# Loading r and k of the first five stages in 1536 B rows, and turning them to head-dim rows on PE through a strided identity

## The chip, the cores and the metric

One core of one Trainium2 chip. Time is device time of one execution in microseconds (us), as the median of several executions. TensorE is called PE, VectorE DVE, ScalarE ACT, GpSimd POOL and SyncE SP. A kernel is compared with the kernel before in the same rounds and on the same chip; ratios are the mean time of one kernel's fast runs over that of the other's fast runs of the same rounds, so they are not quite the ratio of the medians quoted. A run that is more than 1.5% above the fastest of its kernel counts as slow and is left out of ratios.

## The reference, cut to what matters

A linear attention with decay runs over 768 tokens, 8 heads of 48 dims and 4 batches. A two-layer MLP with a leaky ReLU then runs on its 3072 rows.

```python
for t in range(S):                                    # B, H, S, D = 4, 8, 768, 48
    cur = einsum('bhd,bhe->bhde', u * k_t, v_t)       # the "bonus" of the token itself
    y[:, :, t] = einsum('bhd,bhde->bhe', r_t, state + cur)
    state = w * state + einsum('bhd,bhe->bhde', k_t, v_t)
x = y.transpose(0, 2, 1, 3).reshape(3072, 384)
h = x @ w_in                                          # 384 x 2048
out = maximum(0.01 * h, h) @ w_out                    # 2048 x 384
```

The inputs r, k and v lie in memory as [batch, head, token, dim]. For one token and one head there are 48 contiguous fp32 values, 192 B. Eight consecutive tokens of one head are 1536 contiguous bytes.

## The kernel before: what the change and the argument touch

The tokens are worked on in 24 *stages* of 128 tokens, numbered 0 to 23. In each stage r and k are scaled with powers of w, turned so that head dims lie on the partitions (kt), and used for scores, the masked product with v, and the state. Rows y are turned to xT, and the MLP takes them in groups of one or two stages.

```python
# load: partition = token; 128 tokens x 8 heads = 1024 rows of 192 B for each of r, k, v
a = src[b].rearrange("h t d -> t h d")[c * L:c * L + L, :, :]
SP.dma_start(vr.t[:, xi, :, :], a)
# scale (DVE): r * w^(t-128), k * w^(127-t), or the like for the odd stage of a pair
V.tensor_tensor(kq[:, :, 0:D], raw_rk, tab[l], ALU.mult)
# turn (PE): 8 transposes of two heads each, then eviction to kt (DVE or ACT)
PE.transpose(tv[:, 128 * i:128 * i + 128], kq.t[:, 2 * i:2 * i + 2, :], idn)
# scores from kt; y from the masked scores, v and the state; the state from kq (tokens on partitions)
# ... (cut)
```

The tables of powers of w are built at the start from a load of w that is spread over all partitions (192 KB written). The weights of the MLP are loaded by POOL in pieces, each released by an earlier load. All this is data for a small planner inside the program: it simulates the engines and the DMA queues with estimated times and writes down *one fixed order* of operations for each engine.

```python
WI = [4, 4, 8]        # pieces of w_in      WO = [8, 8]   # pieces of w_out
DMA_SEQ = 'st0 st1@w u@k0 uw st2@k0 st3 wi0@u wi1@wi0 wi2@r1 wo0@v3 wo1@wo0'   # x@y: x released by y
MOE_BANKS = 4         # PSUM banks the MLP may hold
...
for _ in range(PASSES):
    P, order = build(landing)             # plans the order, with the landing times of the last pass
    landing, made = P.execute(order)      # simulates it
```

During the first 14 us PE also runs warming matmuls on zeros where the plan has nothing for it.

## Time and profile before

| | before |
|---|---|
| median of 4 runs | 194.53 us (194.17 to 196.57) |
| span of the profiled run | 192.6 us |
| PE busy, idle | 173.0 us, 19.6 us |
| warming matmuls | 9.0 us |
| DVE, ACT, POOL busy | 139.7, 116.7, 78.9 us |
| DMA packets, of them under 512 B | 97,308, 92,296 |

First the page's view of the span in 40 slices of 4.8 us: busy tenths of PE, the granted clock of PE in tenths, the busy share of the DMA engines, and what they moved.

```profile
PE   7875950999999979899899999999999999999973
...
PEclk9999798599999999999999999999999999999999
DMA  5999999999029999999997969996250220110202
GB/s 107 203 164 181 167 206 196 201 189 192 2 85 241 160 223 233 247 192 194 187 200 150 200 112 227 199 177 163 54 118 22 58 82 0 44 43 0 85 0 82
```

The DMA engines are full from the second slice to the tenth, with a gap in the eleventh and twelfth. PE has holes in the sixth and seventh slice (24 to 34 us), and a low clock in the fifth, seventh and eighth.

Next the busy time of each engine by stretch. The columns are: stretch, its length, then busy us (and count) of PE, PE weight loads, DVE, ACT and POOL, then the granted clock, the DMA share and GB/s.

```profile
0.00:35.00 35.00, 22.88 (x272) 17.60 (x273) 19.23 (x44) 13.64 (x26) 8.99 (x19) 0.91 0.95 175
35.00:60.00 25.00, 25.00 (x264) 18.93 (x263) 20.15 (x28) 16.52 (x26) 10.59 (x12) 0.92 0.67 136
60.00:140.00 80.00, 76.64 (x810) 59.89 (x808) 73.29 (x94) 57.28 (x87) 57.66 (x47) 1.00 0.96 185
140.00:200.00 60.00, 48.45 (x436) 36.85 (x432) 26.98 (x36) 29.20 (x40) 1.66 (x2) 0.98 0.15 43
```

PE is idle for 35 - 22.88 = 12.1 us in the first stretch, 0 in the second, 3.4 in the third and, with the span's end at 192.6, 4.2 in the last. From 35 us on PE sets the pace; the start is where time lies.

What the hole is made of stands in the timeline: start, duration, engine, line, operation, and in brackets how long the engine had been idle and what released it.

```profile
18.55 0.71 SPq L554 DMA_DIRECT2D raw<-in_k_dram  x1
...
26.64 0.83 PE L845 MATMUL ps_g<-xT,win 128*128 128x128 bf16 x12
...
32.35 0.96 DVE L653 TENSOR_TENSOR kq<-raw,tab 128x768 bf16<-128x768 f32 x1 [5.95 <-DMA raw<-in_k_dram]
...
33.37 1.04 PE L670 MATMUL ps_g<-idn,kq 128*128 128x128 bf16 x8 [5.89 <-DVE kq L653]
```

PE did nothing between 27.4 and 33.4 us, because the scaled k and r of a stage came late. The load was issued by 19.3 us and k landed at 32.3. After the hole the clock is low: 0.62 of full speed between 35 and 40 us. The Trainium skill, "TensorE: Matmul & The Clock Gate", Part 1, says that PE drops to half rate after an idle window of about 3.4 us and needs as much busy time to come back; the trace agrees for this drop (5.9 us of idle time, then a mean of 0.62). By the trace's clock records PE ran at half speed from 32.0 to 38.8 us. Not every drop follows such a gap: another one, from 18.4 to 21.8 us, came after 3.4 us in which PE was busy for 1.6 us and never idle for more than 0.85 us at a time.

The queues, from the view of the DMA: packets, MB, and the time that the packets took as a share of 16 engines' span.

```profile
q1 hardware_dynamic: 92232, 18.95, 53.7%
...
q10 hardware_dynamic: 3312, 4.52, 7.1%
```

### The profile page before, as it was taken

The page shows a single profiled execution, that of the slowest core. Times are in us where ns is not written, and L with a number is a line of the kernel's source. Part 1 is how long each engine was busy: PE and PEld are TensorE (multiplying, and loading weights), DVE is VectorE, ACT ScalarE, POOL GpSimd, SP SyncE. Part 2 cuts the span into 40 slices and gives each one's busy share as a digit, 9 for nine tenths or more (in the row PEclk, how much of TensorE's full clock was granted, in tenths as well). Part 3 has the DMA queues.
Part 4 walks back from the last instruction along what each step waited for, and adds up shares of the span by engine and source line. Part 5 has one row for each costly group of instructions (what it writes and reads, how often), then busy time and mean ns, then how long its engine had stood idle before and what let it go on. Part 6 is the DMA issues. An engine that isn't in the chain of part 4 may idle for free.

```text
span 192.6 us, 4283 instructions
## 1 busy us (share of the span) xinstructions
PE 173.0 (90%) x1773; PEld 133.3 (69%) x1773; DVE 139.7 (73%) x199; ACT 116.6 (61%) x178; POOL 78.9 (41%) x78
## 2 busy tenths in 40 slices
PE   7875950999999979899899999999999999999973
PEld 5654840597668857767677778778678787796841
DVE  2567942658699989999978997988957847514532
ACT  3844510885746864953975848938939559295450
POOL 2052302820558898958865819956111000000000
PEclk9999798599999999999999999999999999999999
DMA  5999999999029999999997969996250220110202
GB/s 107 203 164 181 167 206 196 201 189 192 2 85 241 160 223 233 247 192 194 187 200 150 200 112 227 199 177 163 54 118 22 58 82 0 44 43 0 85 0 82
DMA packets 97308, 26.90 MB, mean 140 GB/s; under 512 B 92296, under 2 KB 96392, under 8 KB 97288
## 3 DMA queue, kind: packets, MB, share of 16 engines
q1 hardware_dynamic: 92232, 18.95, 53.7%
q0 software_dynamic: 1744, 3.15, 9.3%
q10 hardware_dynamic: 3312, 4.52, 7.1%
q8 instruction: 14, 0.23, 0.5%
q14 instruction: 6, 0.05, 0.1%
HBM read 20.84 MB, written 4.72 MB: 133 GB/s over the span
## 4 chain that ended last, share of the span: by engine, by line
PE 49%; POOL 12%; DVE 10%; DMA 10%; issue 6%; SPq 6%; ACT 4%; ACTq 0%; POOLq 0%; DVEq 0%
PE ps_g L900 23%; PE ps_g L845 19%; DMA raw<-in_v_dram 8%; POOL pr L712 5%; SPq L554 5%; POOL pu L710 4%; DVE gring L880 3%; POOL bv L716 3%; DVE at L746 2%; ACT h L874 2%; DMA lnw<-in_w_dram 2%; DVE kq L653 2%; PE ps_xy L728 2%; PE ps_g L806 1%; PE ps_g L762 1%
## 5 line engine op out<-in xcount | busy, mean ns | idle before, releaser
L845 PE MATMUL ps_g<-xT,win 128*128 128x256 bf16 (+1 forms) x624 | 73.6, 270 | 0.0
L900 PE MATMUL ps_g<-wout,gring 128*128 128x384 bf16 x384 | 67.9, 326 | 4.1 <-DVE gring L880 4.1
L859 ACT ACTIVATE gring<-ps_g 128x512 bf16<-128x512 f32 x96 | 53.3, 597 | 27.7 <-PE ps_g L845 24.5
L845 PEld LDWEIGHTS ps_g<-xT,win 128*128 128x128 bf16 x624 | 61.8, 115 | 2.3 <-issue 0.2
L900 PEld LDWEIGHTS ps_g<-wout,gring 128*128 128x128 bf16 x384 | 35.8, 98 | 27.0 <-DVE gring L880 5.9
L880 DVE TENSOR_TENSOR gring<-gring,h 128x2048 bf16<-128x2048 bf16 (+1 forms) x26 | 34.9, 1341 | 11.8 <-ACT h L874 11.7
L716 POOL TENSOR_TENSOR bv<-vb,b 128x384 bf16<-128x384 bf16 x20 | 20.8, 1038 | 42.4 <-DVE b L714 27.5
L874 ACT ACTIVATE h<-gring 128x2048 bf16<-128x2048 bf16 (+1 forms) x20 | 35.7, 1784 | 0.5
L653 DVE TENSOR_TENSOR kq<-raw,tab 128x768 bf16<-128x768 f32 x24 | 26.0, 1082 | 10.4 <-DMA raw<-in_k_dram 6.6
L746 DVE TENSOR_TENSOR at<-ps_xy,tri 128x1024 bf16<-128x1024 f32 x22 | 26.8, 1216 | 4.7 <-PE ps_xy L728 4.7
L712 POOL TENSOR_TENSOR pr<-pu,raw 128x384 f32<-128x384 f32 x20 | 29.2, 1461 | 1.2
L710 POOL TENSOR_TENSOR pu<-raw,ubc 128x384 f32<-128x384 f32 x20 | 22.8, 1138 | 12.2 <-DMA raw<-in_k_dram 12.2
L657 ACT ACTIVATE vb<-raw 128x384 bf16<-128x384 f32 x24 | 12.6, 525 | 12.4 <-DMA raw<-in_v_dram 11.6
L909 DVE COPY o<-ps_g 128x384 f32<-128x384 f32 x16 | 8.9, 557 | 11.7 <-PE ps_g L900 11.6
L769 DVE TENSOR_TENSOR y<-ps_g,bv 128x384 bf16<-128x384 f32 x24 | 13.2, 549 | 1.5 <-PE ps_g L762 1.3
L812 ACT ACTIVATE xT<-ps_g 128x384 bf16<-128x384 bf16 x14 | 6.8, 487 | 10.6 <-PE ps_g L806 10.6
L714 DVE TENSOR_REDUCE b<-pr 128x8 f32<-128x384 f32 x20 | 10.8, 542 | 2.8 <-POOL pr L712 2.6
L670 PE MATMUL ps_g<-idn,kq 128*128 128x128 bf16 x64 | 5.8, 242 | 7.0 <-DVE kq L653 7.0
L670 PEld LDWEIGHTS ps_g<-idn,kq 128*128 128x128 bf16 x64 | 4.5, 109 | 8.1 <-DVE kq L653 7.6
L924 PE MATMUL ps_g<-zer 128*128 128x256 bf16 x59 | 9.0, 314 | 1.1 <-DVE zer L506 1.1
L728 PE MATMUL ps_xy<-kt 48*128 48x128 bf16 x192 | 10.0, 226 | 0.1
L806 PE MATMUL ps_g<-idn,y 128*128 128x128 bf16 x72 | 8.0, 220 | 2.2 <-DVE y L769 2.1
(56 smaller groups left out, 114.3 us busy)
## 6 DMA issues: line engine op xcount, KB each, us to landing
raw<-in_r_dram SPq DMA_DIRECT2D x24, 192.0 KB, 3.9
raw<-in_k_dram SPq DMA_DIRECT2D x24, 192.0 KB, 4.0
raw<-in_v_dram SPq DMA_DIRECT2D x24, 192.0 KB, 4.1
out_dram<-o ACTq DMA_DIRECT2D x23, 192.0 KB, 3.0
wout<-in_moe_w_out_dram POOLq DMA_DIRECT2D x2, 768.0 KB, 10.4
win<-in_moe_w_in_dram POOLq DMA_DIRECT2D x2, 384.0 KB, 6.7
win<-in_moe_w_in_dram POOLq DMA_DIRECT2D x1, 768.0 KB, 10.4
kt<-kq SPq DMA_TRANSPOSE x16, 3.8
```

The costliest lines, as they stand in the source:

```text
L653: use(op("DVE", 1.0, lambda: V.tensor_tensor(kq.t[:, :, 0:D], vr.t[:, 0:2, :, :].rearrange("p a h d -> p (a h) d"), tab[l][:, :, :, :].rea ...
L710: use(op("POOL", 1.15, lambda: G.tensor_tensor(pu.t[:, :, :], vr.t[:, 1, :, :], ubc[:, :, :], ALU.mult), f"pu{n}", pr_a(n, 0.2), reads=[f_ ...
L712: use(op("POOL", 1.15, lambda: G.tensor_tensor(pr.t[:, :, :], pu.t[:, :, :], vr.t[:, 0, :, :], ALU.mult), f"pr{n}", pr_a(n, 0.3), reads=[f ...
L716: op("POOL", 1.1, lambda: G.tensor_tensor(bv.t[:, :].rearrange("p (h d) -> p h d", d=D), vb.t[:, :].rearrange("p (h d) -> p h d", d=D), bb ...
L728: o = PE.matmul(xy.t[:, 512 * s + 128 * i:512 * s + 128 * i + 128], kt.t[rows, HP + i, :], kt.t[rows, i, :], start=(i == 0), stop=True, sk ...
L746: op("DVE", 1.22, lambda: V.tensor_tensor(at.t[:, :, :], xy.t[:, :].rearrange("p (h t) -> p h t", t=128), tri_b.to_broadcast([128, H, 128] ...
L769: op("DVE", 0.55, lambda: V.tensor_tensor(ys.t[:, :], y.t[:, 0:DM], bv.t[:, :], ALU.add), f"ys{n}", pr_a(n, 0.5), reads=[y, bv], writes=[ys])
L845: o = PE.matmul(bk.t[:, 128 * T * f:128 * T * (f + 1)], w_in_block(s, j * per + f), xT[:, s, L * n0:L * n0 + L * T], start=(s == 0), stop= ...
L859: return A.activation(o_ap, i_ap, AF.Copy) if e == "ACT" else V.tensor_copy(o_ap, i_ap)
L874: return A.activation(o_ap, i_ap, AF.Copy, scale=LRELU_SLOPE)
L880: return V.tensor_tensor(flat(dst(j0, j + 1)), flat(dst(j0, j + 1)), h_ap, ALU.max)
L900: o = PE.matmul(bk.t[:, 0:DM], gring[:, n % NG, fb, :], wout[:, fb, :], start=(fb == 0), stop=(fb == NFB - 1))
```

## The change

The intent is to move the same bytes of r and k of stages 0 to 4 in fewer, longer rows while the DMA engines are full. A 1536 B row holds eight tokens of one head, so a partition is (group of eight tokens, head), which no later step can use directly. Hence new tables for that layout, 16 small matmuls for each of r and k that pick the heads out of the partitions with a strided slice of the identity, an eviction to kt, and for k a second transpose back to token rows, which the state needs.

```diff
-MOE_BANKS = 4                                 +MOE_BANKS = 3
-QKT_DMA_FROM = 8                              +QKT_DMA_FROM = 9
-LEAD = 4.0                                    +LEAD = 5.0
-WI = [4, 4, 8]                                +WI = [4, 4, 4, 4]
-WO = [8, 8]                                   +WO = [4, 4, 8]
-DMA_SEQ = 'st0 st1@w u@k0 uw st2@k0 st3 wi0@u wi1@wi0 wi2@r1 wo0@v3 wo1@wo0'
+DMA_SEQ = 'st0 uw wi0@r0 st1 st2@r0 wi1@v2 wi2 u@r1 w@v0 st3@r1 wi3@v3 wo0@r1 wo1@w wo2'
+NWIDE = 5
-MASK_SPLIT = 2                                +MASK_SPLIT = 0
... (the planner: a margin on landing times, and the mean over four more cases of DMA behaviour)
+        if NWIDE:                             # a small load of w, 48 values a partition, for the wide tables
+            o_wp = op("SP", ..., SP.dma_start(lnp, dram(w, 0, [[0, 16], [D, H], [1, D]])), ...)
... (wide tables: 4 products on DVE, 4 exponentials on ACT; the old tables come later)
+                    if wide:                  # n < NWIDE, r and k only
+                        a = dram(src, (b * H * S + c * L) * D, [[8 * D, 16], [S * D, H], [1, 8 * D]])
+                        return [SP.dma_start(vr.t[:, xi, :, :].rearrange("p h d -> p (h d)"), a)]
... (for x in r, k: kw = raw * wide table, on DVE or POOL)
+                        PE.matmul(tp.t[:, :], zer[:, 0:128], zer[:, :], start=True, stop=False)
+                        for s in range(2):
+                            for j in range(8):
+                                o = PE.matmul(tp.t[64 * s:64 * s + D, 64 * j:64 * j + 64], kw_.t[:, x, j, :],
+                                              idn[:, s:128:2], start=False, stop=True)
... (eviction to kt; for k: 4 transposes of kt back and an eviction to kq)
```

The left and right of a line in the first block stand for a removed and an added line. Several things change at once: row size, engine work, load order, weight pieces and the planner's settings.

More of the change, by code (lines that the diff above doesn't have):

```diff
@@ L28 @@
 NH = 3
-MOE_BANKS = 4
-QKT_DMA_FROM = 8
+MOE_BANKS = 3
+QKT_DMA_FROM = 9
 YT_DMA_FROM = 99
-LEAD = 4.0
+LEAD = 5.0
 PERIOD = 6.0
@@ L39 @@
 RING = 2250
-WI = [4, 4, 8]
-WO = [8, 8]
-DMA_SEQ = 'st0 st1@w u@k0 uw st2@k0 st3 wi0@u wi1@wi0 wi2@r1 wo0@v3 wo1@wo0'
+MARGIN = 0.5
+CASES = [(1.5, 1.08, 1.1, 2.4, 1.35, 1.0), (2.6, 1.0, 1.1, 2.0, 1.6, 1.06), (2.0, 0.95, 1.3, 2.8, 1.9, 1.03), (1.7, 1.04, 1.0, 1.6, 1.2, 0.98)]
+WI = [4, 4, 4, 4]
+WO = [4, 4, 8]
+DMA_SEQ = 'st0 uw wi0@r0 st1 st2@r0 wi1@v2 wi2 u@r1 w@v0 st3@r1 wi3@v3 wo0@r1 wo1@w wo2'
+NWIDE = 5
 BONUS_PE = 4
-MASK_SPLIT = 2
+MASK_SPLIT = 0
 KT_SPLIT = 4
-KQ_SPLIT = 0
+KQ_SPLIT = 1
 GA_ALT = 99
@@ L225, in schedule @@
                 if o.name in self.landing:
-                    o.done = o.end + self.landing[o.name]
+                    o.done = o.end + self.landing[o.name] + (MARGIN if o.name[:2] in ("ld", "wi", "wo") else 0.0)
                 else:
@@ L246, in schedule, with execute @@
         return order
-    def execute(self, order):
+    def execute(self, order, case=(2.0, 1.0, 1.0, 2.4, 1.35, 1.0)):
+        gap_w, cost_l, gap_l, gap_h, land, cost_w = case
         dmaq = {e: [o for o in order[e] if o.pk is not None] for e in ("SP", "POOL", "ACT")}
@@ L303, in issue @@
             heavy = e != "POOL" and any(x in rem and begin[x] <= fin + 1.1 for x in dmaq["POOL"])
-            begin[o] = fin + (2.0 if e == "POOL" else 2.4 if heavy else 1.1)
+            begin[o] = fin + (gap_w if e == "POOL" else gap_h if heavy else gap_l)
             rem[o] = float(o.pk[0])
@@ L322, in live_next @@
             if live:
-                per = sum(o.pk[1] for _, o in live) / 16000.0
+                per = sum(o.pk[1] * (cost_l if o.pk[1] < 50 else cost_w) for _, o in live) / 16000.0
                 t = now + min(rem[o] for _, o in live) * per
@@ L338, in execute @@
             live = [(e, o) for e, o in live if o is not None and o in begin and begin[o] <= now + 1e-9]
-            per = sum(o.pk[1] for _, o in live) / 16000.0
+            per = sum(o.pk[1] * (cost_l if o.pk[1] < 50 else cost_w) for _, o in live) / 16000.0
             for e, o in live:
@@ L344, in execute @@
                 if rem[o] < 1e-6:
-                    done[o] = t + LAND
+                    done[o] = t + land
                     landing[o.name] = done[o] - end[o]
@@ L427, in bass_rwkv5_eagle__then__act_leaky_relu_kernel @@
     lnw = SB("lnw", [128, H, D], FP32)
+    lnp = SB("lnp", [128, D], FP32)
+    row = SB("row", [128, 1], mybir.dt.int32)
+    rowf = SB("rowf", [128, 1], FP32)
+    cj = SB("cj", [128, 2, 2, 8], FP32)
+    tabw = [SB(f"tabw{i}", [128, 2, 8, D], FP32) for i in range(2)]
     ex = SB("ex", [128, 4], FP32)
@@ L437, in bass_rwkv5_eagle__then__act_leaky_relu_kernel @@
     idn = SB("idn", [128, 128])
-    zer = SB("zer", [128, 256])
+    zer = SB("zer", [128, 512])
     gring = SB("gring", [128, NG, NFB, 128])
@@ L444, in bass_rwkv5_eagle__then__act_leaky_relu_kernel @@
         "kt": SBN("kt", NKT, [128, 2 * HP, 128]),
+        "kw": SBN("kw", 2, [128, 2, 8, D]),
         "vb": SBN("vb", NVB, [128, DM]),
@@ L502, in build @@
         f_wo = [fixed(f"wo{i}") for i in range(len(WO))]
-        o_w = op("SP", 0.45, lambda: [SP.dma_start(lnw[:, :, :], dram(w, 0, [[0, 128], [D, H], [1, D]]))],
-                 "w", -200, writes=[f_lnw], pk=(128, 110), sem="w")
+        f_lnp, f_lnp2, f_row, f_rowf = [fixed(x) for x in ("lnp", "lnp2", "row", "rowf")]
+        f_cj = [fixed(f"cj{x}") for x in range(2)]
+        f_tabw = [[fixed(f"tabw{i}{x}") for x in range(2)] for i in range(2)]
+        if NWIDE:
+            o_wp = op("SP", 0.45, lambda: [SP.dma_start(lnp[:, :], dram(w, 0, [[0, 16], [D, H], [1, D]]))],
+                      "wp", -201, writes=[f_lnp], pk=(128, 16.3), sem="wp")
         o_zer = op("DVE", 0.2, lambda: V.memset(zer[:, :], 0.0), "zer", -200, writes=[f_zer])
@@ L528, in build @@
         op("DVE", 0.1, lambda: V.memset(bd[64:128, D:2 * D], 1.0), "bd2", -178, writes=[f_bd])
-        op("ACT", 0.52, lambda: A.activation(lnw[:, :, :], lnw[:, :, :], AF.Ln), "ln", -190, reads=[f_lnw], writes=[f_lnw2])
-        for i in range(2):
-            for j in range(2):
-                op("ACT", 0.6, (lambda i=i, j=j: A.activation(tab[i][:, j, :, :], lnw[:, :, :], AF.Exp,
-                                                              scale=ex[:, 2 * i + j:2 * i + j + 1])),
-                   f"tab{i}{j}", -180 + 4 * i + j, reads=[f_lnw2, f_ex[2 * i + j]], writes=[f_tab[i][j]])
+        if NWIDE:
+            op("POOL", 0.14, lambda: G.iota(row[:, :], pattern=[[0, 1]], base=0, channel_multiplier=1), "row", -199.9,
+               writes=[f_row])
+            for x, (base, sg) in enumerate([(-L, 1), (L - 1, -1)]):
+                op("POOL", 0.14, (lambda x=x, base=base, sg=sg: G.iota(
+                    cj[:, :, x, :], pattern=[[sg * L, 2], [sg, 8]], base=base, channel_multiplier=0,
+                    allow_small_or_imprecise_dtypes=True)), f"cj{x}", -199.8 + 0.01 * x, writes=[f_cj[x]])
+            op("DVE", 0.07, lambda: V.tensor_scalar(row[:, :], row[:, :], 120, None, ALU.bitwise_and), "rowa", -199,
+               writes=[f_row])
+            op("DVE", 0.07, lambda: V.tensor_copy(rowf[:, :], row[:, :]), "rowf", -198, reads=[f_row], writes=[f_rowf])
+            for x in range(2):
+                op("DVE", 0.1, (lambda x=x: V.tensor_scalar(cj[:, :, x, :], cj[:, :, x, :], rowf[:, 0:1], None,
+                                                            (ALU.add, ALU.subtract)[x])), f"cja{x}", -197,
+                   reads=[f_rowf], writes=[f_cj[x]])
+            op("ACT", 0.2, lambda: A.activation(lnp[:, :], lnp[:, :], AF.Ln), "lnp", -196, reads=[f_lnp], writes=[f_lnp2])
+            for i in range(min(2, NWIDE)):
+                for x in range(2):
+                    op("DVE", 0.5, (lambda i=i, x=x: V.tensor_tensor(
+                        tabw[i][:, x, :, :], cj[:, i, x, :].unsqueeze(2).to_broadcast([128, 8, D]),
+                        lnp[:, :].unsqueeze(1).to_broadcast([128, 8, D]), ALU.mult)), f"tw{i}{x}", -195 + 10 * i + x,
+                       reads=[f_lnp2, f_cj[x]], writes=[f_tabw[i][x]])
+                    op("ACT", 0.52, (lambda i=i, x=x: A.activation(tabw[i][:, x, :, :], tabw[i][:, x, :, :], AF.Exp)),
+                       f"te{i}{x}", -195 + 10 * i + x, writes=[f_tabw[i][x]])
@@ L537, in build @@
+        op_w = lambda gates: op("SP", 0.45, lambda: [SP.dma_start(lnw[:, :, :], dram(w, 0, [[0, 128], [D, H], [1, D]]))],
+                                "w", -184, writes=[f_lnw], after=gates, pk=(128, 110), sem="w")
+        seq0 = DMA_SEQ.split()
+        o_w = op_w([]) if "w" not in [x.partition("@")[0] for x in seq0] else None
         puw = bank("a_uw")
@@ L550, in load, with go @@
                 fv = fixed(f"{nm}{n}")
-                def go(xi=xi, src=src):
+                wide = n < NWIDE and xi < 2
+                def go(xi=xi, src=src, wide=wide):
+                    if wide:
+                        a = dram(src, (b * H * S + c * L) * D, [[8 * D, 16], [S * D, H], [1, 8 * D]])
+                        return [SP.dma_start(vr.t[:, xi, :, :].rearrange("p h d -> p (h d)"), a)]
                     a = src[b].rearrange("h t d -> t h d")[c * L:c * L + L, :, :]
                     return [SP.dma_start(vr.t[:, xi, :, :], a)]
-                o = op("SP", 0.47, go, f"ld{nm}{n}", prio + 0.01 * xi, writes=[fv], pk=(1024, 16.3),
+                o = op("SP", 0.47, go, f"ld{nm}{n}", prio + 0.01 * xi, writes=[fv], pk=(128, 68) if wide else (1024, 16.3),
                        after=after if xi == 0 else (), behind=parts[-1:])
@@ L578, in wo_load @@
                       f"wo{i}", -140 + i, writes=[f_wo[i]], after=after, pk=(128 * n, 248), sem=f"wo{i}")
-        last = {"SP": o_w, "POOL": None}
+        last = {"SP": o_w or o_wp, "POOL": None}
         def chain(o, e):
+            o = o or P.ops[-1]
             if last[e] is not None:
@@ L585, in chain @@
             last[e] = P.ops[-1]
-        for item in DMA_SEQ.split():
+        for item in seq0:
             name, _, gate = item.partition("@")
@@ L596, in build @@
                          "r": lambda: loads[gn][0:1], "k": lambda: loads[gn][1:2], "v": lambda: loads[gn][2:3],
-                         "w": lambda: [o_w], "u": lambda: f_u.writers[:1]}[gk]()
-            if kind == "u":
+                         "w": lambda: f_lnw.writers[:1], "u": lambda: f_u.writers[:1]}[gk]()
+            if kind == "w":
+                op_w(gates)
+                chain(None, "SP")
+            elif kind == "u":
                 chain(op("SP", 0.4, lambda: [SP.dma_start(ubc[:, :, :], dram(u, 0, [[0, 128], [D, H], [1, D]]))],
@@ L618, in build @@
                 chain(P.ops[m], "SP")
-        op("PE", 0.3, go_tuw, "tuw", -150, reads=[f_wu, f_id4], writes=[puw]).count = 2
+        pt = -190 if not NWIDE else (NWIDE - LEAD - 2) * PERIOD
+        op("ACT", 0.52, lambda: A.activation(lnw[:, :, :], lnw[:, :, :], AF.Ln), "ln", pt, reads=[f_lnw], writes=[f_lnw2])
+        for i in range(2):
+            for j in range(2):
+                op("ACT", 0.6, (lambda i=i, j=j: A.activation(tab[i][:, j, :, :], lnw[:, :, :], AF.Exp,
+                                                              scale=ex[:, 2 * i + j:2 * i + j + 1])),
+                   f"tab{i}{j}", pt + 0.1 + 0.2 * i + 0.1 * j, reads=[f_lnw2, f_ex[2 * i + j]], writes=[f_tab[i][j]])
+        op("PE", 0.1, go_tuw, "tuw", -150, reads=[f_wu, f_id4], writes=[puw]).count = 2
         op("DVE", 0.17, lambda: V.tensor_copy(wcol[:, :], puw.t[:, 0:HP]), "wc", -100, reads=[puw], writes=[f_wc])
@@ L645, in attention, with mw, go_w, cpw @@
             kq = new("kq", n)
-            if n < KQ_SPLIT:
+            kt = new("kt", n)
+            if n < NWIDE:
+                kw_ = new("kw", n)
+                for x in range(2):
+                    kws = {"writes": [kw_]} if x == 0 else {"joins": [kw_]}
+                    def mw(eng, x=x):
+                        return eng.tensor_tensor(kw_.t[:, x, :, :].rearrange("p j d -> p (j d)"),
+                                                 vr.t[:, x, :, :].rearrange("p h d -> p (h d)"),
+                                                 tabw[l][:, x, :, :].rearrange("p j d -> p (j d)"), ALU.mult)
+                    mo = op("DVE", 0.55, (lambda mw=mw: mw(V)), f"kw{n}_{x}", pr_a(n, 0.0),
+                            reads=[(f_r, f_k)[x], f_tabw[l][x]], alt=("POOL", 1.15, (lambda mw=mw: mw(G))) if n else None, **kws)
+                    use(mo)
+                    tp = bank(f"a_tw{n}_{x}")
+                    def go_w(x=x, tp=tp):
+                        PE.matmul(tp.t[:, :], zer[:, 0:128], zer[:, :], start=True, stop=False, skip_group_check=True)
+                        o = None
+                        for s in range(2):
+                            for j in range(8):
+                                o = PE.matmul(tp.t[64 * s:64 * s + D, 64 * j:64 * j + 64], kw_.t[:, x, j, :], idn[:, s:128:2],
+                                              start=False, stop=True, skip_group_check=True)
+                        return o
+                    q = op("PE", 0.7, go_w, f"tw{n}_{x}", pr_a(n, 0.2 + 0.05 * x), reads=[f_idn], writes=[tp], after=[mo, o_zer])
+                    q.count = 17
+                    kw_.readers.append(q)
+                    def cpw(e, x=x, tp=tp):
+                        o_ap = kt.t[:, HP * x:HP * x + HP, :].rearrange("p a (g j) -> p a g j", j=8)
+                        i_ap = tp.t[:, :].rearrange("p (j g a) -> p a g j", g=16, a=HP)
+                        return V.tensor_copy(o_ap, i_ap) if e == "DVE" else A.activation(o_ap, i_ap, AF.Copy)
+                    kws = {"writes": [kt]} if x == 0 else {"joins": [kt]}
+                    ev = op("DVE", 0.69, (lambda cpw=cpw: cpw("DVE")), f"kt{n}_{x}", pr_a(n, 0.3), reads=[tp],
+                            alt=("ACT", 0.6, (lambda cpw=cpw: cpw("ACT"))), **kws)
+                bk = bank(f"a_bk{n}")
+                def go_bk():
+                    o = None
+                    tv = bk.t[:, :].bitcast(BF16)
+                    for i in range(HP):
+                        o = PE.transpose(tv[:, 128 * i:128 * i + 128], kt.t[:, HP + i, :], idn[:, :])
+                    return o
+                q = op("PE", 0.22, go_bk, f"bk{n}", pr_a(n, 0.47), reads=[f_idn], writes=[bk], after=[ev])
+                q.count = HP
+                kt.readers.append(q)
+                def cpb(e):
+                    o_ap = kq.t[:, H:2 * H, :].rearrange("p h e -> p (h e)")
+                    i_ap = bk.t[:, :].bitcast(BF16)[:, 0:512]
+                    return V.tensor_copy(o_ap, i_ap) if e == "DVE" else A.activation(o_ap, i_ap, AF.Copy)
+                op("DVE", 0.42, lambda: cpb("DVE"), f"kq{n}", pr_a(n, 0.48), reads=[bk] + f_pad, writes=[kq],
+                   alt=("ACT", 0.6, lambda: cpb("ACT")))
+            elif n < KQ_SPLIT:
@@ L658, in attention @@
                    f"vb{n}", pr_a(n, 0.1), reads=[f_v], writes=[vb]))
-            kt = new("kt", n)
-            if n < QKT_DMA_FROM:
+            if n < NWIDE:
+                pass
+            elif n < QKT_DMA_FROM:
                 parts = 2 if n < KT_SPLIT else 1
@@ L702, in go_pb @@
                     return o
-                op("PE", 0.15, go_pb, f"pb{n}", pr_a(n, 0.42), reads=[pq, f_uw], writes=[pb]).count = HP
+                op("PE", 0.09, go_pb, f"pb{n}", pr_a(n, 0.42), reads=[pq, f_uw], writes=[pb]).count = HP
                 op("DVE", 0.56, lambda: V.tensor_tensor(bv.t[:, :].rearrange("p (h d) -> p h d", d=D),
@@ L765, in go_y @@
                 return o
-            op("PE", 0.38, go_y, f"y{n}", pr_a(n, 0.5), reads=[kt, at, vb] + ([sprev] if sprev else []), writes=[y])
+            op("PE", 0.38 if sprev is not None else 0.21, go_y, f"y{n}", pr_a(n, 0.5), reads=[kt, at, vb] + ([sprev] if sprev else []), writes=[y])
             ys = new("y", n)
@@ L931, in bass_rwkv5_eagle__then__act_leaky_relu_kernel @@
         landing, made = P.execute(order)
+        made += sum(P.execute(order, case)[1] for case in CASES)
+        made /= 1 + len(CASES)
         if VERBOSE:
```

## The prediction

> **What bounds the kernel now.** Two phases. From 5 to 47 us the DMA engines are full (40 slices: DMA share 9 nearly throughout, 164 to 206 GB/s) while PE does little: by the timeline it has finished only attention of stages 0 to 2 and the first-layer matmuls of stage 0 by 35.2 us, some 7 us of useful work; the rest is warming matmuls (L924, 9.0 us), a granted clock of 0.62 to 0.84 in 15 to 25 and 30 to 40 us, and idle time (the largest, 5.9 us before L670 at 33.4, waits for k of stage 3; one load took 14.8 us to land beside the weight loads). From 35 to 183 us PE is 93 to 100% busy (table by stretches): PE-bound, DVE close behind at 92% until 140. The last 10 us are a serial tail. So the time is when PE gets dense, and with how much done.
>
> **Removed.** Queue 1: 92,232 packets, mostly of 192 B, took 53.7% of 16 engines' 192.6 us: 17.9 ns each, so a 1024-row load costs about 1.15 us. The stores (queue 10: 3,312 packets, mostly 1536 B, 7.1%) took 66 ns each, so a 128-row load should cost 0.53 us (estimate). Ten loads: about 6 us less DMA time in a full phase. The Trainium skill, "DMA: Bandwidth & Descriptors", Specifications, asks for at least 512 B per transfer for line rate; 92,296 of the trace's 97,308 packets are below. The wide table of w at the head gives way to a small one. Weights in smaller pieces, the first released by r of stage 0 (now issued at 11.3, landed at 18.4 us), should let first-layer matmuls start at 12 to 15 us, not 19.0. The POOL mask (1.39 us) goes; the small w/u load, and so the first bonus (now at 13.1), moves forward.
>
> **Added, per wide stage.** PE: two times 17 matmuls (0.75 us, estimated from L762, eight in 0.20 us, and a 512-column zeroing of about 0.22) plus 4 transposes back (0.22), less 8 transposes (0.45): +1.3 us, 6.5 in all, four fifths of it in time now idle or filler. DVE/ACT: two products of 0.55 for one of 0.96, two fp32 evictions of 0.65 for 0.42+0.60, one more of 0.42: +0.8 us. A stage's chain gets longer by a transpose and eviction before the state update. Tables take four products and four exponentials, so stage 0's scores hardly come earlier (8.6 now). Three PSUM banks, not four, for the MLP is a small risk.
>
> **Sum.** PE dense from about 24 to 27 us, with some 11 us of today's useful work done, where today that is reached at about 39. That is up to 13 us; less 1.5 for PE work left over and a few for DVE/ACT latency. I expect 9.
>
> **Prediction: 185.3 us, 179.5 to 191. Faster by over 2%: 0.80; within 2%: 0.15; slower: 0.05.**
>
> **What would show it.** Packets near 88,300; first-layer matmuls from 12 to 15 us; the 5.9 us wait gone; PE busy in 15 to 35 us about doubled; less filler; the stretch from 60 to 180 us as dense as now; the tail unchanged.
>
> **What would make it wrong.** Wide loads not much cheaper; weights starved by the SP queue; the strided eviction or small matmuls far dearer; DVE, not PE, pacing from 25 us on, so that the lead is lost by 140; three banks leaving PE waiting for ACT.
>
> Stage 4 is wide but takes its bonus from raw r and k as if rows were tokens: wrong by a small term, it seems, not in time.

## The result, and the profile after

The changed kernel takes 187.59 us (median of 4, 187.26 to 187.83) against 194.53 us of the kernel before, a ratio of 0.9621 (95% interval 0.9553 to 0.9689). That is 6.9 us by the medians. The prediction was 185.3 us with a range of 179.5 to 191.

```profile
PE   7749979999899999989999999999999999999983
...
PEclk9957999999999999999999999999999999999999
DMA  3899999889992779899989699998250020110202
GB/s 94 141 266 268 214 212 210 174 165 238 216 211 80 136 151 261 168 199 208 192 196 103 129 207 198 185 172 202 60 139 4 4 85 4 45 40 0 88 0 85
```

The holes of PE in the sixth and seventh slice are gone, and so is the low clock after them; a half clock from 9.3 to 16.1 us has come instead.

```profile
0.00:35.00 35.00, 28.29 (x464) 22.48 (x469) 26.91 (x61) 21.91 (x42) 13.80 (x28) 0.90 1.00 201
35.00:60.00 25.00, 24.32 (x259) 19.05 (x257) 20.03 (x26) 16.58 (x28) 15.37 (x13) 1.00 0.84 180
60.00:140.00 80.00, 78.92 (x824) 60.67 (x822) 71.42 (x91) 57.18 (x90) 54.81 (x45) 1.00 0.92 169
140.00:200.00 60.00, 41.40 (x356) 31.64 (x353) 21.93 (x28) 24.00 (x35) 0.00 (x0) 0.99 0.08 27
```

PE's busy time is what it was (172.9 us), since the added matmuls stand where warming matmuls (now 5.3 us) and slowly clocked matmuls stood. All of the gain is idle time: 19.6 us before, 12.6 now. By stretch it went from 12.1, 0, 3.4 and 4.2 us to 6.7, 0.7, 1.1 and 4.1 us. So 5.4 us come from the first 35 us and 2.3 us from the stretch between 60 and 140 us, which I had expected to stay as it was.

The early timeline shows what went as predicted and what did not:

```profile
5.19 1.02 DVE L704 TENSOR_TENSOR kw<-raw,tabw 128x384 bf16<-128x384 f32 x2
...
7.75 0.56 PE L717 MATMUL ps_g<-idn,kw 128*48 128x64 bf16 x16
...
9.76 0.56 DVE L704 TENSOR_TENSOR kw<-raw,tabw 128x384 bf16<-128x384 f32 x1 [2.50 <-DMA raw<-in_r_dram]
...
10.71 0.68 DVE L727 CAST kt<-ps_g 128x512 bf16<-128x512 f32 x1
...
13.87 0.60 PE L832 MATMUL ps_xy<-kt 48*128 48x128 bf16 x8
...
19.25 0.86 PE L949 MATMUL ps_g<-xT,win 128*128 128x128 bf16 x12
...
23.53 2.10 DVE L704 TENSOR_TENSOR kw<-raw,tabw 128x384 bf16<-128x384 f32 x3
```

Stage 0's k is turned on PE by 8.3 us (the second L717 at 7.75). Its eviction waits on DVE until 10.71, because the order has the product of stage 1 in front of it, and that waits until 9.76 for r of stage 1. The scores follow at 13.87 and the first first-layer matmuls at 19.25, no earlier than the 19.03 of before. I had expected 12 to 15 us. The last line is the product of stage 3's k and of both of stage 4 (one line of 3): the loads of stage 4 are now in use at 24 us, where before they were in use at 32.4.

```profile
q1 hardware_dynamic: 82216, 18.52, 54.3%
```

### The profile page after: what moved, and what is told of

Same layout as the page of the kernel before. It is cut to its first block, busy times and chain, and to the rows that moved or that the text cites. A ratio compares the mean times of both kernels' runs of the same rounds, so it can differ in the third digit from the quotient of the medians.

```text
span 185.5 us, 4583 instructions
## 1 busy us (share of the span) xinstructions
PE 172.9 (93%) x1893; PEld 133.8 (72%) x1897; DVE 140.3 (76%) x203; ACT 119.7 (65%) x193; POOL 84.0 (45%) x85
## 2 busy tenths in 40 slices
DMA packets 87853, 26.68 MB, mean 144 GB/s; under 512 B 81176, under 2 KB 87320, under 8 KB 87832
## 4 chain that ended last, share of the span: by engine, by line
PE 60%; DVE 13%; issue 10%; ACT 9%; POOL 5%; DMA 1%; ACTq 0%; POOLq 0%
PE ps_g L1004 25%; PE ps_g L949 24%; DVE gring L984 4%; ACT h L978 4%; PE ps_xy L832 3%; DVE at L850 2%; ACT gring L963 2%; POOL pr L816 2%; DVE kq L756 2%; PE ps_g L910 2%; PE ps_g L866 1%; DVE y L873 1%; PE ps_g L717 1%; PE ps_st L889 1%; POOL bv L820 1%
## 5 line engine op out<-in xcount | busy, mean ns | idle before, releaser
L820 POOL TENSOR_TENSOR bv<-vb,b 128x384 bf16<-128x384 bf16 x20 | 24.5, 1226 | 39.0 <-DVE b L818 24.4
L984 DVE TENSOR_TENSOR gring<-gring,h 128x2048 bf16<-128x2048 bf16 (+1 forms) x26 | 32.1, 1237 | 10.3 <-ACT h L978 10.0
L850 DVE TENSOR_TENSOR at<-ps_xy,tri 128x1024 bf16<-128x1024 f32 x24 | 29.2, 1217 | 6.8 <-PE ps_xy L832 6.7
L978 ACT ACTIVATE h<-gring 128x2048 bf16<-128x2048 bf16 (+1 forms) x18 | 32.1, 1781 | 0.4
L756 DVE TENSOR_TENSOR kq<-raw,tab 128x768 bf16<-128x768 f32 x19 | 22.4, 1177 | 0.0
L1012 ACT ACTIVATE o<-ps_g 128x384 f32<-128x384 f32 x13 | 6.4, 491 | 17.5 <-PE ps_g L1004 17.5
L1013 DVE COPY o<-ps_g 128x384 f32<-128x384 f32 x11 | 6.1, 558 | 10.2 <-PE ps_g L1004 10.1
L977 DVE TENSOR_SCALAR h<-gring 128x2048 bf16<-128x2048 bf16 (+1 forms) x8 | 6.3, 783 | 7.0 <-ACT gring L963 7.0
L717 PE MATMUL ps_g<-idn,kw 128*48 128x64 bf16 x160 | 6.3, 205 | 3.4 <-DVE kw L704 2.9
L866 PE MATMUL ps_g<-vb,at 128*128 128x48 bf16 x192 | 8.7, 183 | 0.0
```

Of the source, the lines that this page charges most:

```text
L756: use(op("DVE", 1.0, lambda: V.tensor_tensor(kq.t[:, :, 0:D], vr.t[:, 0:2, :, :].rearrange("p a h d -> p (a h) d"), tab[l][:, :, :, :].rea ...
L820: op("POOL", 1.1, lambda: G.tensor_tensor(bv.t[:, :].rearrange("p (h d) -> p h d", d=D), vb.t[:, :].rearrange("p (h d) -> p h d", d=D), bb ...
L850: op("DVE", 1.22, lambda: V.tensor_tensor(at.t[:, :, :], xy.t[:, :].rearrange("p (h t) -> p h t", t=128), tri_b.to_broadcast([128, H, 128] ...
L978: return A.activation(o_ap, i_ap, AF.Copy, scale=LRELU_SLOPE)
L984: return V.tensor_tensor(flat(dst(j0, j + 1)), flat(dst(j0, j + 1)), h_ap, ALU.max)
```

## The experiments

Twelve kernels ran. Six of them differ from their parent in the loads alone or in a few operations, with the fixed order of everything else untouched; these carry the argument. In the other six a setting or a rule of the planner changes and it writes a new order, which by itself moves the time. The kernel before took 193.7 to 194.7 us (medians) in the different rounds, so differences of medians from different rounds are good to about 1 us; the ratios are the safer measure. Theory A says that the row size brings the gain; the rival B says that the new order, the weight pieces and the settings bring it.

### Row size alone, in the changed program

```diff
                     if wide:
-                        a = dram(src, ..., [[8 * D, 16], [S * D, H], [1, 8 * D]])
-                        return [SP.dma_start(vr.t[:, xi, :, :].rearrange("p h d -> p (h d)"), a)]
+                        pass        # falls through to the 192 B rows; values wrong on purpose
```

The instruction streams of PE, DVE, ACT and POOL were compared and are the same.

> The changed kernel with one edit: r and k of the first five stages are loaded in 192 B rows again, while every instruction of PE, DVE, ACT and POOL and its order stay the same (values come out wrong on purpose). Theory A, the row size brings the gain: the ten loads cost 1.15 us of DMA time again, not about 0.5, PE waits in the first 35 us come back, 191.5 to 195 us. Rival B, the new order, the weight pieces and the planner's settings bring the gain: 187 to 189.5 us, as the changed kernel.

Measured: 191.11 us (190.28 to 193.44, one of four runs slow), ratio to before 0.9814 (0.971 to 0.9918), where the changed kernel has 0.9621. So the 1536 B rows are worth 3.5 us by the medians in this program, and the intervals of the two ratios do not overlap. The time lies a little below A's range, and outside B's.

```profile
0.00:35.00 35.00, 24.80 (x403) 19.34 (x408) 24.00 (x55) 18.50 (x37) 12.82 (x27) 0.90 0.91 168
35.00:60.00 25.00, 24.27 (x262) 19.06 (x260) 19.89 (x28) 16.39 (x27) 12.63 (x11) 1.00 1.02 210
60.00:140.00 80.00, 79.02 (x843) 60.97 (x842) 72.63 (x92) 57.77 (x92) 56.22 (x47) 1.00 0.89 168
140.00:200.00 60.00, 44.98 (x392) 34.63 (x390) 24.34 (x32) 27.04 (x39) 2.22 (x2) 0.99 0.11 35
```

Against the changed kernel, 35 - 24.80 = 10.2 us of PE are idle in the first stretch instead of 6.7, which is the whole difference; the stretch from 60 to 140 us is as dense as there (79.02 and 78.92). How the loads fared shows in a window in which both programs work through the same list of loads, from 9.7 to 19 us. The DMA view of the changed kernel there, with packets and bytes in all, then queue 1 alone with the time that its packets took:

```profile
DMA packets 4559, 2.50 MB, mean 269 GB/s; under 512 B 3260, under 2 KB 4558, under 8 KB 4558
...
q1 hardware_dynamic: 4356, 2.29, 101.4%
```

And of this one:

```profile
DMA packets 7353, 1.87 MB, mean 201 GB/s; under 512 B 6943, under 2 KB 7352, under 8 KB 7352
...
q1 hardware_dynamic: 7183, 1.70, 88.5%
```

In the same 9.3 us the wide rows brought 2.50 MB, the narrow ones 1.87 MB. Worked out by size from the packet records of the two traces, in the first 35 us a row of 1536 B on queue 1 took 89.8 ns in the changed kernel, and a row of 192 B took 16.2 ns in this run. On 16 engines that makes 0.72 us for a load in wide rows and 1.04 us for one in narrow rows.

The loads are also issued at other times. This is the issue of k of stage 4, first in the changed kernel:

```profile
15.16 0.61 SPq L591 DMA_DIRECT2D raw<-in_k_dram  x1
```

And in this one, with the product that uses it:

```profile
20.49 2.98 SPq L593 DMA_DIRECT2D raw<-in_k_dram  x1
...
27.64 0.56 DVE L704 TENSOR_TENSOR kw<-raw,tabw 128x384 bf16<-128x384 f32 x1 [0.19 <-DMA raw<-in_k_dram]
```

With narrow rows SP is held for 3.78, 4.40 and 2.98 us in three of its issues, where in the changed kernel each issue of r, k or v up to here takes 0.5 to 0.7 us. So k of stage 4 is issued 5.3 us later, and it lands at 27.6 instead of 20.9 us. When a load is issued matters: in each program of this pair and the next, two or three loads that were issued beside the bulk of the weight loads landed only 13.7 to 16.7 us after their issue. Wide rows can thus help in two ways, by less packet time and by bringing stage 4's r and k in ahead of the weights; no run separates the two.

### Row size alone, in the kernel before

The mirror: the kernel before, with nothing but the access pattern of the first ten loads of r and k changed.

> The mirror: the kernel before, every instruction and its order the same, but r and k of the first five stages loaded in 1536 B rows (values wrong on purpose). Theory A: 188 to 191.5 us, with no PE work added. Rival B: 193 to 195.5, the loads land sooner but the old order gives nothing back.

Measured: 187.86 us (186.48 to 188.40), ratio 0.9652 (0.9578 to 0.9726). Loads in wide rows, with no added work and no new order, bring 5.8 us by the medians, nearly what the whole change brings. (It can't be used: the values are wrong.)

```profile
0.00:35.00 35.00, 28.44 (x369) 23.16 (x370) 24.99 (x52) 20.86 (x37) 9.28 (x20) 0.95 0.89 186
35.00:60.00 25.00, 23.91 (x244) 18.14 (x243) 22.96 (x30) 15.04 (x27) 15.29 (x14) 1.00 0.95 182
60.00:140.00 80.00, 76.61 (x795) 59.05 (x793) 69.93 (x88) 55.46 (x81) 52.74 (x44) 1.00 0.92 174
140.00:200.00 60.00, 41.82 (x375) 31.57 (x372) 23.71 (x31) 25.30 (x36) 0.83 (x1) 0.98 0.10 32
```

From its timeline, the issue of k of stage 4, and the operation that was the line at 32.35 us before:

```profile
13.76 1.59 SPq L554 DMA_DIRECT2D raw<-in_k_dram  x1
...
27.05 0.94 DVE L653 TENSOR_TENSOR kq<-raw,tab 128x768 bf16<-128x768 f32 x1
```

That k was issued at 18.55 us before and took 13.8 us to land; here it is issued at 13.76 and lands 7.0 us later, at 20.8. Idle time of the first stretch falls from 12.1 to 6.6 us and the stage whose data came at 32.3 us is now scaled at 27.05. The stretch from 60 to 140 us stays as it was before (76.61 and 76.64). PE is busy 2.2 us less in all, with the same instructions, because the low clock after the hole is gone: PE is at half speed for 3.4 us in the first 40 us here, and for 10.2 us before.

### The settings without the rows, and the rows without the settings

```diff
 # the settings alone                          # the rows with the settings of before
-NWIDE = 5                                     -MOE_BANKS = 3, LEAD = 5.0, MARGIN = 0.5, CASES = [...]
+NWIDE = 0                                     +MOE_BANKS = 4, LEAD = 4.0, MARGIN = 0.0, CASES = []
 # w table loaded first, as before             # WI, WO, MASK_SPLIT, QKT_DMA_FROM, KQ_SPLIT and load order
                                                # as before, but for the big w table (later)
```

> The changed kernel's settings (weight pieces, order of loads with the w table first, planner with cases, three banks for the MLP, lead 5), but no wide stage. Theory A: 191.5 to 196 us. Rival B: 187 to 190 us.

> Five wide stages with the settings of the kernel before (old weight pieces and order of loads, four banks, lead 4, no cases and no margin). Theory A: 186 to 190.5 us. Rival B: 191.5 to 196 us, since the added PE work of some 1.2 us a stage is not paid for by the loads alone.

Measured: the settings alone 196.43 us, ratio 1.0095 (1.0019 to 1.0171); the rows with the old settings 191.56 us, ratio 0.9849 (0.9782 to 0.9916). The settings alone bring no gain, which speaks against B. The rows with the old settings fall at the edge of B's range: with the work that the layout needs, and an order planned for other settings, only 2.1 us of the 5.8 are left. It would fit that the settings of the change pay for the added work, but both are newly planned orders, and the weight of that comes out below; so this is not shown.

### Stage 0 ahead of stage 1

Sixteen operations at the start are moved after planning, so that stage 0's chain no longer stands in line behind a product that waits for stage 1's r. This is the part of the prediction that had failed.

```diff
+    for e, after, names in (("DVE", "kt0_1", "pq0 at0 bv0 s0 ys0 kw1_0 kt1_0"),
+                            ("PE", "tw0_1", "sc0 bk0 pb0 kv0 y0 yt0"),
+                            ("ACT", "kt0_0", "kq0 xt0"), ("PE", "tw1_1", "g1_0_0")):
+        for nm in names.split(): move(e, nm, after); after = nm
```

> The changed kernel, only the order of eleven operations near the start edited after planning: on DVE, PE and ACT all of stage 0's chain now stands ahead of stage 1's first product (which waits for r of stage 1, landed at 9.7 us, where the plan had 7.3), and stage 0's first first-layer matmuls ahead of stage 2. Theory C, part of the expected gain (9 us, measured 7) was lost because stage 0 stood in line behind stage 1: first-layer matmuls from 13 to 15 us (19.3 now) and 184.5 to 187 us. Rival D: the start of the first layer is not what binds, the loads and weights are: 187 to 188.5 us, same as the changed kernel.

Measured: 187.34 us (187.09 to 188.74), ratio 0.9643 (0.9604 to 0.9683), and the values were wrong, which was not meant (relative error 0.072). (The text speaks of eleven operations; the edit names sixteen.) The cause of the wrong values that I proposed: three warming matmuls, which the planner puts into the order without tying them to a PSUM bank, now came after the moved first-layer matmuls and overwrote the bank. The next version moves those three to the front as well.

> The unblocked order once more with three warming matmuls moved ahead of the moved first-layer matmuls, whose PSUM bank they overwrite in the earlier attempt (it gave wrong values). Values right to the tolerance if that was the cause. Time as there, 187 to 188 us (rival D), not 184.5 to 186.5 (theory C).

Measured: values right, 187.16 us (186.60 to 189.72, one of four runs slow), ratio 0.9603 (0.9545 to 0.9661). That confirms the cause, and the time is again that of the changed kernel. Its first-layer matmuls of the start:

```profile
15.47 1.47 PE L949 MATMUL ps_g<-xT,win 128*128 128x128 bf16 x12
...
23.80 0.86 PE L949 MATMUL ps_g<-xT,win 128*128 128x128 bf16 x12
...
28.20 0.84 PE L949 MATMUL ps_g<-xT,win 128*128 128x128 bf16 x12
```

And those of the changed kernel:

```profile
19.25 0.86 PE L949 MATMUL ps_g<-xT,win 128*128 128x128 bf16 x12
...
22.66 0.84 PE L949 MATMUL ps_g<-xT,win 128*128 128x128 bf16 x12
...
27.85 0.84 PE L949 MATMUL ps_g<-xT,win 128*128 128x128 bf16 x12
```

The first group starts 3.8 us sooner; the second already 1.1 us later, the third 0.35 later. The prediction's step "first-layer matmuls from 12 to 15 us" was wrong, but it cost nothing: that early start is given back by 24 us.

The same idea left to the planner:

```diff
+                    mo.behind.update(wide_gate.get(n - 1, ()))   # products after the last stage's evictions
+                    q.behind.update(sc_gate.get(n - 1, ()))      # matmuls after the last stage's scores
```

> The same idea left to the planner: a wide stage's products and matmuls are planned only after the previous stage's evictions and scores; the whole order is planned anew. Theory C: 184.5 to 187 us. Rival D: 187 to 189 us. A new plan alone may move it by some 2 us either way.

Measured: 190.23 us (two of five runs slow, and the profile fell on one of them, so it is not read here), ratio of the fast runs 0.9771 (0.974 to 0.98). It is slower than the changed kernel.

### Less of the added PE work

```diff
                         for s in range(2):
-                            for j in range(8):
+                            for j in range(1):      # values wrong on purpose, same order
```

> The changed kernel, same order, but each transpose through the strided identity does 2 of its 16 matmuls (values wrong on purpose), which takes some 0.45 us away ten times, 4.5 us of PE work. My prediction had most of this work in idle time: 186 to 187.5 us. Rival, the PE work is paid in full: 183 to 184 us.

Measured: 186.14 us (185.63 to 187.05), ratio 0.9572 (0.9539 to 0.9605) against 0.9621. Fourteen of sixteen matmuls gone, ten times, bring about 1 to 1.5 us; the intervals of the two ratios overlap, so not even that is sure. In the trace of the changed kernel sixteen such matmuls take 0.56 us warm, so some 10 x 0.56 x 14/16 = 4.9 us of PE work were removed. The net gain is in the predicted range. It is not a clean measure of how much had been hidden, for the clock changed too: in the profiled run, the slowest of the four, PE is at half speed from 8.2 to 21.8 us, where it is from 9.3 to 16.1 us in the changed kernel. Part of what the removed work gave may have gone into that; the two fast runs with the changed kernel's mean clock took 185.63 and 186.25 us.

### v in wide rows too

```diff
-                    if wide:
+                    if n < NWIDE:        # v as well; values wrong on purpose, same order
```

> The changed kernel, same order, but v of the first five stages in 1536 B rows too (values wrong on purpose, nothing else changes). Theory E, the start is still bound by the DMA engines after the change: 1.5 to 3.5 us faster than the changed kernel, 184 to 186 us. Rival F, it is bound by the chain of small operations on PE, DVE and ACT: 187 to 188 us.

Measured: 187.34 us (187.11 to 187.45), ratio 0.962 (0.9575 to 0.9665), the same as the changed kernel. Five more loads in wide rows bring nothing: theory E falls, and the price of these loads no longer sets the pace of the start. The third first-layer group starts at 27.92 us here and at 27.85 in the changed kernel. What is full in both between 15 and 35 us is DVE, with PE close behind; the changed kernel:

```profile
15.00:20.00 5.00, 4.64 (x94) 3.77 (x92) 4.34 (x8) 3.51 (x8) 3.11 (x5) 0.89 1.15 240
20.00:25.00 5.00, 3.92 (x78) 2.98 (x76) 5.00 (x9) 5.00 (x12) 4.20 (x6) 1.00 1.23 209
25.00:30.00 5.00, 4.75 (x110) 4.23 (x110) 4.72 (x9) 2.62 (x6) 0.00 (x0) 1.00 1.13 210
30.00:35.00 5.00, 4.95 (x91) 4.52 (x87) 4.56 (x9) 4.78 (x8) 1.18 (x1) 1.00 1.08 208
```

DVE is busy 18.6 of these 20 us and all of the second five; PE is busy 18.3 and ACT 15.9. That DVE sets the pace is a reading of the profile, with the three nulls (loads, early first layer, PE work nearly so) on its side; no run took DVE work away, so it is argued and not shown. It also leaves much open: of the 6.7 us that PE still idles in the first 35 us, 5.0 us lie before 15 us, where DVE is busy for 8.3 of 15 us, and PE is at half speed from 9.3 to 16.1 us.

### Values of stage 4, and new plans

Stage 4 is wide, but its bonus is still taken on POOL from raw r and k as if partitions were tokens (the bonus goes to PE for stages below 4 only). Worked out on the reference's data with that bonus put in the wrong layout, the result is off by 0.012 in relative norm, and by 0.060 in the 128 rows of stage 4. The tolerance lets that pass, yet it is a defect. Two mended versions, and one that also gives the planner better issue times:

```diff
 # mended on PE          # mended by width       # mended, with issue times of the trace
-BONUS_PE = 4            -NWIDE = 5              -BONUS_PE = 4, load 0.47 us, w/u loads 0.80 us
+BONUS_PE = 5            +NWIDE = 4              +BONUS_PE = 5, load 0.60 us, w/u loads 1.45 us
```

> The changed kernel with the bonus of stage 4 taken on PE too, which mends its values (stage 4 takes its bonus from raw r and k in the wrong layout); planned anew. 186 to 189.5 us: one POOL product chain less, 0.4 us DVE and some PE more.

> Four wide stages, which makes all values right; planned anew. By the row size alone (3.5 us for ten loads in the changed program) two loads less cost 0.7 us, and the PE work saved is worth about 0.3: 187 to 190 us.

> Five wide stages, the bonus of stage 4 mended, and the planner told the issue times that the trace shows (0.60 us a load, 1.45 us for the two w/u loads, where it assumed 0.47 and 0.80). If the plan's wrong landing times cost time: 185 to 187.5 us, better than the mended kernel's 188.8; if not, 187.5 to 190.

Measured: 188.82 us, ratio 0.9709 (0.9683 to 0.9736); 188.63 us, ratio 0.9692 (0.9633 to 0.9752); 189.89 us, ratio 0.9762 (0.9703 to 0.9821). The better issue times made the plan no better: that hypothesis falls. The mended kernels are still about 3% faster than before, 1.0 to 1.2 us behind the changed one. The stretch that tells why, of the kernel mended on PE:

```profile
60.00:140.00 80.00, 77.45 (x798) 58.80 (x796) 71.50 (x90) 53.40 (x87) 52.67 (x43) 1.00 0.90 172
```

PE is idle 80 - 77.45 = 2.6 us there. In the changed kernel it is 1.1, in the kernel before 3.4, and in the other newly planned ones 2.8 (rows with old settings), 4.7 (settings alone), 2.2 (four wide stages) and 3.7 (with issue times). The 2.3 us that the change gains between 60 and 140 us go with this one order: a single setting that touches one stage at the start took 1.5 of them away.

No version beat the changed kernel beyond the width of the intervals.

## Why the prediction was right, point by point

The time lay in the range, and the direction was right; the gain was 6.9 us where I had 9.

- **What bounds the start: right, with a wrong name.** The hole before 33.4 us was the cost, and wide rows close it. Both pairs with a fixed order show it: first-stretch idle time 12.1 to 6.6 us in the old program and 10.2 to 6.7 in the new one. What the prediction did not have is that the load came late by being issued late, beside the weights. The load that PE waited for was k of stage 4, not of stage 3.
- **"a 128-row load should cost 0.53 us ... about 6 us less DMA time": right in direction, too large.** I had taken the price of a wide row from the stores (66 ns) and that of a narrow one from the mean of queue 1 (17.9 ns, which includes the 256 B packets of the transposing loads, 25.7 ns each). By size, narrow rows took 16.1 ns in the first 35 us of the kernel before, wide ones 83.4 ns in its mirror and 89.8 ns in the changed kernel. The time of all packets of 192 and 1536 B on queue 1 fell by 52 us in the changed program (1,203 to 1,151) and by 59 us in the old one (1,218 to 1,159): 3.3 and 3.7 us on each of 16 engines. The total of queue 1 does not show it (1,611 and 1,612 us in the changed program), because the transposing loads took 390 us in the one trace and 445 in the other; and traces of programs with the very same loads range from 1,526 (stage 0 ahead of stage 1, first try) to 1,684 us (less PE work). The packet count itself came as said, 87,853 for "near 88,300": one transposing load less takes 1,024 away, and more weight pieces add some.
- **"First-layer matmuls from 12 to 15 us": wrong, and of no account.** The planned order held stage 0 behind stage 1, on DVE until 10.7 us and on PE until 13.9 us. Putting it right on the chip brought the start to 15.5 us and no time.
- **"up to 13 us": the term that was mis-sized.** I had PE dense from 24 to 27 us with as much done as today at 39. PE was dense from 25 us (4.75 of the next 5 us), but by 35 us it had finished 101 of the 624 first-layer matmuls and no second-layer ones. Before, it had finished 90 by 41 us and 103 by 42. So it stood where the old one stood at 41.8 us, a lead of 6.8 us; counted in columns, since matmuls of 128 and of 256 columns are mixed, it is 5.9 us. It was not 12 to 15. Something besides the loads holds the start, for which DVE at 93% from 15 to 35 us is a candidate and no more; the 5.0 us of idle time before 15 us stay unexplained by it.
- **"1.5 for PE work left over": right in size, as far as known.** Taking most of the added matmuls away brought 1 to 1.5 us, net of what a lower clock took back. Each transpose with its zeroing comes 0.81 us after the last (25.07, 25.88 and 26.69 us in the changed kernel), for my 0.75.
- **"the stretch from 60 to 180 us as dense as now": wrong by 2.3 us to the good.** This is a property of the one order that the planner found, not of the rows. It made up for part of what the start fell short.
- **PE busy in 15 to 35 us "about doubled":** 10.9 us became 18.3, 1.7 times. Warming matmuls fell from 9.0 to 5.3 us, and the tail stayed (4.2 and 4.1 us idle), as said.

So the size came out near by two errors of opposite sign: the lead of the start was too large, and the gain in the middle was not foreseen. That part of the nearness is luck.

## What to carry to other kernels

Where a start is bound by loads of short rows, test the row size alone first: change only the access pattern, accept wrong values, and keep every instruction where it was. It tells in one run what the layout alone brings (5.8 us here), before anyone writes the work that it needs. And where a planner writes the order anew at every change of a setting, a few us of any comparison can belong to the order (1 to 3 us here); pairs with the order held fixed are the ones to argue from.

## What the Trainium skill lacked or had wrong

- "DMA: Bandwidth & Descriptors", Specifications: it states at least 512 B for line rate, and the runs agree in direction. Its measured table is for loads issued from GpSimd, by size; no measured rate is given for loads issued from SP in rows of 192 B beside 1536 B (only a fixed overhead for each small descriptor, from which one might be estimated). Runs: 16.2 ns for a row of 192 B and 89.8 ns for one of 1536 B in the first 35 us, and 1.87 and 2.50 MB in the same 9.3 us of the same program, three queues mixed.
- The same page, "Queues, rings and completion order": it says that an engine takes turns between queues packet by packet. A packet there is a group of descriptors, where the trace counts each row as one, so the page does not say whether longer rows win a larger share beside the weight loads. No run here separates that from a lower cost per byte: in that window the weights' queue moved 0.19 MB beside wide rows and 0.16 beside narrow ones.
- "Perfetto Trace Analysis", Identifying the Most-Contended Engine: it warns that occupancy of 16 DMA engines misleads. The runs show how far: packet time of queue 1 from 1,526 to 1,684 us in programs with the same loads, and shares above 1 (1.23 between 20 and 25 us). The prediction priced the loads by such means and should have heeded the page.
- "TensorE: Matmul & The Clock Gate", LDWEIGHTS: it gives the columns over 1.2 ns, so 48 columns should take less than half of 128. The trace records 103 ns (median) for the 48-column loads of the new matmuls and 98 ns for the 128-column loads of the transposes back, but the records overlap: at 25 us the former start 23 ns apart on average, at 28.5 us the latter 56 ns apart. So the starts agree with the page, and the length of one record is no measure of a load's cost.
- No page that I drew on says how long a load may wait behind weight loads: v of stage 4 took 14.8 us from issue to landing in the kernel before, and k of stage 5 took 16.7 us in the changed one.
- No page says how busy PE must be within a window to keep its clock. The runs show half speed after windows of 3.4 us in which PE was busy for 1.6 us (at 18.4 us before) and 2.1 us (at 9.3 us in the changed kernel), with no gap in them longer than 1.0 us.
